# Gated linear attention into two mixture layers on one core: the transposed keys share pY's bank, POOL's selection comes after the state's scaling, the words of w_in are fetched later, and y has three buffers

## The chip, the cores and the metric

The kernel runs on one core of a Trainium2 chip. The metric is the device time of one execution in microseconds (us), and lower is better. The engines are named as in the profile: PE (TensorE, with PEld for its weight loads), DVE (VectorE), ACT (ScalarE), POOL (GpSimd) and SP (the queue that issues the DMAs). Each engine works through its own instructions in program order and waits on semaphores for the others.

## What is computed

The reference has three parts. The change lies in the first one and in the preparation of one weight of the third.

```python
# attention: B=4, H=8, S=768, D=48, a state of 48x48 per head
f = 1/(1+exp(-f_logit))
for t in range(S):
    state = f[t][:,None]*state + outer(k[t], v[t])
    y[t]  = q[t] @ state
x = y.transpose(0,2,1,3).reshape(3072, 384)
# first mixture layer: 8 experts, each takes its 384 best tokens
logits = x @ w_gate ; greedy assignment by logit ; out = relu(x@w1[e]) @ w2[e]
# second layer: one dense pair of weights
h = x @ w_in ; out = (h*clip(h+3,0,6)/6) @ w_out
```

## The kernel before

`gla_moe_ffn` first runs `attention` (until about 190 us of the span), then routes the tokens and runs eight experts, whose matmuls fill PE until the end.

**Units and chunks.** Attention cuts each batch's 768 steps into units of 384 and chunks of 128. There are 8 units and 24 chunks. A unit has three chunks, and one round of the main loop (lines 232 to 262) handles chunk j while it prepares a third of the next unit's data. A round with `ti==2` is the last of its unit: there POOL also rearranges the next unit's q and k (`reorder`, line 66), some 2.5 us each, and ACT its f (line 65).

**What a round does.** Four groups `tg(0)` to `tg(3)` each transpose one head pair of f, q or k into a bank pT (PE, line 81). ACT turns f into `ff` (line 85), and DVE makes running products `P` (93) and `S` (91) and scales q and k by them into `qt` (105) and `kh` (98). Between these groups stand the matmuls of the chunks:

- `l_mm(j-1)`, line 195: the finished y of the chunk before is transposed to rows and multiplied with w_gate, into bank pM. ACT copies `y` out (line 200), DVE reduces the logits `lg` (197), and SP stores y to x_dram (201). `y` has two buffers.
- `y_mm(j,0)`, line 163: the state `St` times q, into bank pY. The first chunk of a sequence has none.
- `a_mm(j+1)`, line 135: the next chunk's scores, into banks pA0 and pA1. ACT copies them to `am` (line 140), and POOL zeroes what lies after the step, with an affine select in place (line 141, `a_ev`).
- `y_mm(j,1)`, line 169: the scores times v, added in pY. ACT copies the result to `yt` (171).
- `kv_mm(j)`, line 181: the transposed keys `kt` times v, into pK. DVE adds that to the state (188, or 186 in the first chunk), POOL scales the state (189). This pair is the closure `update`, appended to the list `late`.
- `kt_mm(j+1)`, line 148: the keys of the next chunk are transposed into bank pM, and ACT copies them to `kt` (149). The last chunk of a sequence has none, so 20 of 24 rounds have one.

The function `group` runs what was left over from the group before, calls one step of `prep` as a filler, and at its end everything in `late`, in order. Eight banks of PSUM are in use: three pT, pA0, pA1, pM, pY and pK, one buffer each.

```python
            tg(0)
            if 0<=j-1<NCH: l_mm(j-1)
            tg(1)
            if 0<=j<NCH: y_mm(j,0)
            a_mm(j+1); a_ev(j+1,0); a_ev(j+1,1)
            if 0<=j<NCH: y_mm(j,1)
            if j>=0: kv_mm(j)
            tg(2)
            if j+1<NCH: kt_mm(j+1)
            tg(3)
```

**The preparation of w_in.** `narrowed` (from line 858) is a generator that is stepped by the groups. The weight arrives as 64-bit words, twelve blocks of 512 KB. For each block, ACT takes an absolute value into `pm` (line 872), DVE does four integer steps (882, 884, 886, 889), of which the last writes `pw`, ACT rounds to `wih` (line 669), and POOL subtracts for `wil` (line 670). `pw` has two buffers, and the block after next is fetched (line 867) at once behind that subtraction, whose end SP then awaits.

Of the kernel before, what the change touches and what calls it, by code (L numbers as in the profile page):

```python
# [10 lines left out]
F32=mybir.dt.float32; F32R=mybir.dt.float32r; BF=mybir.dt.bfloat16; I32=mybir.dt.int32; U32=mybir.dt.uint32  # L11
AF=mybir.ActivationFunctionType; OP=mybir.AluOpType; AX=mybir.AxisListType
PS=bass.MemoryType.PSUM
B,H,S,D=4,8,768,48
C=128; U=384; NP=4; NU=B*S//U; NCH=B*S//C
PMIN=2.0**-60; PB=3; MB=1

def attention(tc, q,k,v,f,wg, x_dram, lg, ident, pmin, ranges, prep, setup, spin):
    nc=tc.nc
    ctx=ExitStack()  # L20
    with ctx:
        ld=ctx.enter_context(tc.tile_pool(name="ald",bufs=2))
        cs=ctx.enter_context(tc.tile_pool(name="acs",bufs=1))
        wk=ctx.enter_context(tc.tile_pool(name="awk",bufs=2))
        ps=ctx.enter_context(tc.tile_pool(name="aps",bufs=1,space=PS))
# [42 lines left out]
        def tgroup(u,p,nm):  # L68
# [14 lines left out]
            if nm=='f':  # L83
# [3 lines left out]
                P2=PP[u,p//2]; P=P2[:,p%2]; pp=slice(p-1,p+1)  # L87
                V=nc.vector; ends=lambda t: t.rearrange("p a (c t) -> p a c t",t=C)[:,:,:,C-1]
                def suffix():
                    SS[u,p]=wk.tile([128,U],F32,name="S",bufs=3)  # L90
                    V.tensor_tensor_scan(SS[u,p][:,::-1],ff[:,1:U+1][:,::-1],m1[:,p%2,::-1],1.0,op0=OP.mult,op1=OP.max)
                SF[u,p]=suffix
                ops=[lambda: V.tensor_tensor_scan(P,m0,ff[:,:U],1.0,op0=OP.max,op1=OP.mult)]
                if p%2==0: return ops,[]
                return (ops+[lambda: V.tensor_scalar(PC[u][:,pp],ends(P2),PMIN,None,op0=OP.max)],
                        [lambda: V.reciprocal(ends(m1),PC[u][:,pp]),SF[u,p-1]])
            elif nm=='k':
# [38 lines left out]
        def a_ev(j,s):  # L136
            if s==0:
                AM[j]=wk.tile([128,2,NP,C],F32,name="am")
            am=AM[j][:,s]
            nc.scalar.copy(am,pA[j][s])  # L140
            nc.gpsimd.affine_select(out=am,in_=am,pattern=[[0,NP],[1,C]],compare_op=OP.is_ge,fill=0.0,base=0,channel_multiplier=-1)
        def kt_mm(j):
            u,c=divmod(j,3)
            if j%6==5: return
            kt=wk.tile([128,4,2,64],F32,name="kt")
            pk=ps.tile([128,NP,128],F32,name="pM",bufs=MB)
            for p in range(NP):
                nc.tensor.transpose(pk[:,p],KH[u][:,p,c*C:(c+1)*C],ident)
            nc.scalar.copy(kt.rearrange("p a s d -> p a (s d)"),pk)
            KT[j]=kt  # L150
# [22 lines left out]
        def kv_mm(j):  # L173
            u,c=divmod(j,3); first=j%6==0
            if j%6==5 or j>=NCH: return
            vr=raw['v',u]
            bank=ps.tile([128,512],F32,name="pK")
            pk=bank[:,:NP*D].rearrange("p (a d) -> p a d",a=NP)
            for p in range(NP):
                for s in range(2):  # L180
                    nc.tensor.matmul(pk[64*s:64*s+64,p],KT[j][:,p,s],vr[:,c,2*p+s,:D],start=True,stop=True)
            sn=St[(j+1)%2][:,:,:D]; so=St[j%2][:,:,:D]
            def update():
                pcb=PC[u][:,:,c][:,:,None].to_broadcast([128,NP,D])
                if first:
                    nc.vector.tensor_tensor(out=sn,in0=pk,in1=pcb,op=OP.mult)
                else:
                    nc.vector.tensor_add(so,so,pk)
                    nc.gpsimd.tensor_tensor(out=sn,in0=so,in1=pcb,op=OP.mult)
            late.append(update)  # L190
        def l_mm(j):
            W=2*D+8
            px=ps.tile([128,512],F32,name="pM" if j<NCH-1 else "pK",bufs=MB)[:,:NP*W].rearrange("p (a e) -> p a e",a=NP)
            for p in range(NP):
                nc.tensor.matmul(px[:,p],YT[j][:,p],SW[:,p],start=True,stop=True)  # L195
            y=wk.tile([128,NP,2*D],F32,name="y")
            def logits(): nc.vector.tensor_reduce(lg[:,j],px[:,:,2*D:].rearrange("p a e -> p e a"),axis=AX.X,op=OP.add)
            if j==NCH-1: logits()
            else: late.append(logits)
            nc.scalar.copy(y,px[:,:,:2*D])  # L200
            later.append(lambda: nc.sync.dma_start(x_dram[j*C:(j+1)*C,:],y.rearrange("p a d -> p (a d)")))
# [32 lines left out]
        for j in range(-1,NCH+1):  # L234
            tu,ti=divmod(j+1,3)
            tu+=1
            g=[(tu,)+x for x in ORD[4*ti:4*ti+4]] if tu<NU else [None]*4
            if j>=0 and j%3==0 and j//3+1<NU: load(j//3+1,'v')
            def tg(i):
                group(tgroup(*g[i]) if g[i] is not None else ([],[]),(lambda: next(prep,None)) if j>=0 and i in PREP[ti] else None,(ti,i)==(2,3))  # L240
            if j==NCH: spin(lambda: ps.tile([128,384],F32,name="pT",bufs=PB),TAIL[0])
            tg(0)
            if 0<=j-1<NCH: l_mm(j-1)
            if j==NCH: spin(lambda: ps.tile([128,384],F32,name="pT",bufs=PB),TAIL[1])
            tg(1)
            while later: later.pop(0)()
            if ti==2: refill(tu+1,'f')
            if 0<=j<NCH: y_mm(j,0)
            if j+1<NCH:
                a_mm(j+1)  # L250
                a_ev(j+1,0)
                a_ev(j+1,1)
            if 0<=j<NCH: y_mm(j,1)
            if j>=0: kv_mm(j)
            tg(2)
            if j+1<NCH: kt_mm(j+1)
            if ti==2: refill(tu+1,'q')
            tg(3)
            if ti==2: refill(tu+1,'k')
            if j>=0: next(constants,None)  # L260
            if j>=NCH-4: next(ranges,None)
            if j in (17,22,24): next(early)
            if 0<=j<10: next(prep,None)
# [54 lines left out]
class Routing:  # L318
# [60 lines left out]
    def spin(s,tile,n):  # L379

        if not n: return
        t=tile()
        for _ in range(n): s.tc.nc.tensor.matmul(t[:,:128],s.ones,s.before,start=True,stop=True)  # L383
# [23 lines left out]
    def phase(s,k):  # L407
        nc=s.tc.nc; V=nc.vector
        b24=lambda x: x[:,:,None].to_broadcast([128,NT,E])
# [258 lines left out]
def split_raw(nc, raw, hi, lo, eng_lo):  # L668
    nc.scalar.copy(hi, raw)  # L669
    eng_lo.tensor_tensor(out=lo, in0=raw, in1=hi.bitcast(F32), op=OP.subtract)  # L670
# [175 lines left out]
def gla_moe_ffn(tc,q,k,v,f_logit,moe_w_gate,moe_w1,moe_w2,moe2_w_in,moe2_w_out,out):  # L846
    nc=tc.nc
    with ExitStack() as ctx:
# [6 lines left out]
        nc.vector.memset(pmin,1.0)  # L855
        rwk=ctx.enter_context(tc.tile_pool(name="rwk",bufs=1))
        wih=cs.tile([128,3,F2],F32R,name="wih"); wil=cs.tile([128,3,F2],F32R,name="wil")
        def narrowed(pool,jobs,W,work,places):

            words=jobs[0].dtype!=F32  # L860
            got={}; mag={}
            def fetch(i):
                if i>=len(jobs): return
                n=jobs[i].shape[-1]
                w=pool.tile([128,W,2],U32,name="pw",bufs=2)
                if not words: w=w.rearrange("p c t -> p (c t)")[:,:n].bitcast(F32)
                nc.sync.dma_start(w.rearrange("p c t -> p (c t)") if words else w,jobs[i].bitcast(U32) if words else jobs[i])
                got[i]=w
            def absolute(i):
                if not words or i>=len(jobs): return  # L870
                mag[i]=work(i)
                nc.scalar.activation(mag[i],got[i][:,:,1].bitcast(F32),AF.Abs)
            fetch(0); fetch(1)
            yield
            absolute(0)
            for i in range(len(jobs)):
                yield
                r=got[i]
                if words:
                    V=nc.vector  # L880
                    lw,hw=got[i][:,:,0],got[i][:,:,1]; m=mag[i]; t=m.bitcast(U32)
                    V.tensor_scalar(m,m,2.0**-15,None,op0=OP.max)
                    yield
                    V.tensor_scalar(t,t,3,0x3ffffff8,op0=OP.logical_shift_left,op1=OP.bitwise_and)
                    yield
                    V.scalar_tensor_tensor(t,hw,0xC0000000,t,op0=OP.bitwise_and,op1=OP.bitwise_or)
                    yield
                    absolute(i+1)
                    V.scalar_tensor_tensor(lw,lw,29,t,op0=OP.logical_shift_right,op1=OP.bitwise_or)
                    r=lw.bitcast(F32)  # L890
                hi,lo=places(i)
                split_raw(nc,r,hi,lo,nc.gpsimd)
                fetch(i+2)
        def prep_in(pool):
            cc=lambda i: slice(i%4*512,i%4*512+512)
            return narrowed(pool,[moe2_w_in[i//4*128:i//4*128+128,cc(i)] for i in range(12)],512,
                            lambda i: pool.tile([128,512],F32,name="pm",bufs=2),
                            lambda i: (wih[:,i//4,cc(i)],wil[:,i//4,cc(i)]))
        wol={}
        def prep_out(pool):  # L900
            def places(g):
# [134 lines left out]
```

## Time and profile before

| | us |
|---|---|
| median of 3 runs | 896.9 (895.48 to 900.68) |
| the profiled execution | 900.39 |
| its span in the trace | 898.7 |
| PE busy over the span | 837.9 (93%) |
| DVE busy | 534.9 (60%) |
| ACT busy | 371.1 (41%) |
| POOL busy | 307.8 (34%) |
| granted clock of PE, mean | 0.968 |

The profile is of one execution. Busy shares are averages over attention, routing and experts, which have different limits, so what a change in attention is worth is read from the stretch of attention alone. The granted clock is given as a share: 1.00 is 2.4 GHz and 0.50 is 1.2 GHz. A row of the timeline gives the start in us from the span's start, the duration, the engine, the line, the operation and its tiles; in brackets stands the idle time of that engine just before the row, and what ended it.

### The profile page before, as it was taken

What the parts mean: (1) busy time and instruction counts of PE and PEld (TensorE: products, weight loads), DVE (VectorE), ACT (ScalarE), POOL (GpSimd) and SP (SyncE); (2) the same over time, 40 slices, a digit from 0 to 9 for tenths busy, and PEclk for the clock granted to TensorE, in tenths of its full rate; (3) what the DMA queues carried; (4) which work ended last, traced back from release to release, by engine and by line L of the source; (5) the groups of instructions that cost most, each with busy time, mean ns of one, the idle gap of its engine ahead of it and who ended that gap; (6) DMA issues with size and microseconds to landing.
All of it is one profiled execution on the core that took longest, in us unless ns stands there. A gap on an engine that the chain in (4) does not pass through costs nothing.

```text
span 898.7 us, 16095 instructions
## 1 busy us (share of the span) xinstructions
PE 837.9 (93%) x6086; PEld 788.9 (88%) x6086; DVE 534.9 (60%) x1369; ACT 371.1 (41%) x741; POOL 307.8 (34%) x378
## 2 busy tenths in 40 slices
PE   7998889896987699999999999999999999999995
PEld 5887778786877699989999999999999999999995
DVE  7989799567768844674574565555674422431331
ACT  4655556424234441542354144316423541642331
POOL 7677566316213540432133133313330440331001
PEclk9999899977999899999999999999999999999998
DMA  8775686026123411120221112201220220110000
GB/s 257 189 167 125 172 237 144 29 78 187 53 71 101 119 62 37 63 71 27 74 62 33 63 62 63 71 27 58 61 77 12 75 91 18 60 47 27 1 1 31
DMA packets 77158, 71.91 MB, mean 80 GB/s; under 512 B 29200, under 2 KB 65040, under 8 KB 77072
## 3 DMA queue, kind: packets, MB, share of 16 engines
q1 hardware_dynamic: 74000, 61.37, 24.0%
q0 software_dynamic: 3072, 9.44, 3.3%
q8 instruction: 49, 0.80, 0.4%
q14 instruction: 37, 0.30, 0.1%
HBM read 61.35 MB, written 9.44 MB: 79 GB/s over the span
## 4 chain that ended last, share of the span: by engine, by line
PE 57%; issue 14%; DVE 7%; ACT 2%; POOL 2%; DMA 2%; SPq 0%; POOLq 0%; ACTq 0%; DVEq 0%
PE pF L673 9%; PE acc L673 9%; PE pF L675 8%; PE pF L674 8%; PE acc L675 8%; PE acc L674 8%; POOL wol L670 1%; DVE ga L806 1%; PE pM L195 1%; PE pA L135 1%; DMA pw<-in_moe_w_out_dram 1%; PE pY L169 1%; PE pY L163 1%; PE acc L383 1%; POOL out_dram L838 1%
## 5 line engine op out<-in xcount | busy, mean ns | idle before, releaser
L806 DVE SCALAR_TENSOR_TENSOR ga<-ga,pF 128x384 f32<-128x384 f32 x128 | 70.7, 552 | 109.5 <-ACT ga L805 109.3
L673 PE MATMUL pF<-xh,wih 128*128 128x384 f32 x384 | 133.3, 347 | 1.9 <-ACT xh L790 1.9
L673 PE MATMUL acc<-woh,hh 128*128 128x384 f32 x384 | 134.2, 349 | 0.0
L675 PE MATMUL pF<-xl,wih 128*128 128x384 f32 x384 | 131.3, 342 | 0.0
L674 PE MATMUL pF<-xh,wil 128*128 128x384 f32 x384 | 130.9, 341 | 0.0
L674 PE MATMUL acc<-woh,hl 128*128 128x384 f32 x384 | 130.0, 339 | 0.9 <-DVE hl L809 0.9
L675 PE MATMUL acc<-wol,hh 128*128 128x384 f32 x384 | 130.0, 338 | 0.0
L670 POOL TENSOR_TENSOR w1l<-wst,w1h 128x512 fp32r<-128x512 f32 x42 | 55.6, 1323 | 173.9 <-ACT w1h L669 173.9
L805 ACT ACTIVATE ga<-pF,three 128x384 f32<-128x384 f32 x128 | 74.1, 579 | 99.2 <-PE pF L675 99.1
L809 DVE TENSOR_TENSOR hl<-ga,hh 128x384 fp32r<-128x384 f32 x128 | 72.8, 569 | 60.2 <-ACT hh L808 59.9
L808 ACT CAST hh<-ga 128x384 fp32r<-128x384 f32 x128 | 65.7, 513 | 104.0 <-DVE ga L806 104.0
L670 POOL TENSOR_TENSOR w2l<-wst,w2h 128x384 fp32r<-128x384 f32 x58 | 59.9, 1035 | 111.5 <-ACT w2h L669 111.5
L771 ACT ACTIVATE hh<-pF 128x384 fp32r<-128x384 f32 x64 | 31.4, 492 | 123.1 <-PE pF L675 111.9
L772 DVE SCALAR_TENSOR_TENSOR hl<-pF,hh 128x384 fp32r<-128x384 f32 x64 | 35.5, 555 | 75.1 <-ACT hh L771 74.8
L673 PEld LDWEIGHTS pF<-xh,wih 128*128 128x128 f32 x384 | 73.0, 190 | 2.3 <-ACT xh L790 2.2
L674 PEld LDWEIGHTS acc<-woh,hl 128*128 128x128 f32 x384 | 72.7, 189 | 1.3 <-DVE hl L809 1.3
L675 PEld LDWEIGHTS pF<-xl,wih 128*128 128x128 f32 x384 | 73.3, 191 | 0.4 <-DVE xl L791 0.3
L674 PEld LDWEIGHTS pF<-xh,wil 128*128 128x128 f32 x384 | 73.2, 191 | 0.0
L673 PEld LDWEIGHTS acc<-woh,hh 128*128 128x128 f32 x384 | 72.7, 189 | 0.1
L675 PEld LDWEIGHTS acc<-wol,hh 128*128 128x128 f32 x384 | 72.6, 189 | 0.0
L673 PE MATMUL pF<-xh,w1h 128*128 128x384 f32 x192 | 67.8, 353 | 0.6 <-ACT xh L741 0.6
L675 PE MATMUL acc<-hl,w2h 128*128 128x384 f32 x192 | 64.5, 336 | 3.0 <-DVE hl L772 3.0
(286 smaller groups left out, 1766.8 us busy)
## 6 DMA issues: line engine op xcount, KB each, us to landing
wst<-in_moe_w_dram SPq DMA_DIRECT2D x58, 192.0 KB, 2.4
wst<-in_moe_w_dram SPq DMA_DIRECT2D x42, 256.0 KB, 2.7
pw<-in_moe_w_in_dram SPq DMA_DIRECT2D x12, 512.0 KB, 4.0
pw<-in_moe_w_out_dram SPq DMA_DIRECT2D x16, 384.0 KB, 3.1
v<-in_v_dram SPq DMA_DIRECT2D x24, 192.0 KB, 5.2
x_dram<-y SPq DMA_DIRECT2D x24, 192.0 KB, 3.6
fr<-in_f_logit_dram SPq DMA_DIRECT2D x7, 576.0 KB, 5.4
kr<-in_k_dram SPq DMA_DIRECT2D x7, 576.0 KB, 5.6
```

The source lines that it names most:

```text
L135: nc.tensor.matmul(pA[j][s][:,p],KH[u][r,p,c*C:(c+1)*C],QT[u][r,p,c*C:(c+1)*C],start=True,stop=True)
L163: for r in rows: nc.tensor.matmul(PY[j][p//2][r,p],St[j%2][r,p],QT[u][r,p,cc],start=p==0 or last and p==2,stop=False)
L670: eng_lo.tensor_tensor(out=lo, in0=raw, in1=hi.bitcast(F32), op=OP.subtract)
L673: nc.tensor.matmul(out, ahi, bhi, start=start, stop=False)
L674: nc.tensor.matmul(out, alo, bhi, start=False, stop=False)
L675: nc.tensor.matmul(out, ahi, blo, start=False, stop=stop)
L771: nc.scalar.activation(hh,p,AF.Relu)
L772: s.defer(2,lambda: nc.vector.scalar_tensor_tensor(hl,p,0.0,hh.bitcast(F32),op0=OP.max,op1=OP.subtract))
L805: nc.scalar.activation(a,p,AF.Relu,bias=s.three[:,0:1])
L806: late(f,1,lambda: nc.vector.scalar_tensor_tensor(g,a,6.0,p,op0=OP.min,op1=OP.mult))
L808: late(f,1,lambda: nc.scalar.copy(gh,g))
L809: late(f,3,lambda: nc.vector.tensor_tensor(out=gl,in0=g,in1=gh.bitcast(F32),op=OP.subtract))
```

## The change

There are four edits. `kt_mm` moves from the end of a round (for the next chunk) to the next round, behind `tg(0)` and ahead of `l_mm`, and its transposes go into bank pY and not into pM. The affine select is no longer issued in `a_ev` but put into `late`, and `update` goes to the front of `late`, so that POOL scales the state first. The words of w_in's block i+1 are fetched when the work on block i begins, which is one step of the generator later than before. `y` gets a third buffer.

```diff
@@ a_ev
             nc.scalar.copy(am,pA[j][s])
-            nc.gpsimd.affine_select(out=am,in_=am,pattern=[[0,NP],[1,C]],compare_op=OP.is_ge,fill=0.0,base=0,channel_multiplier=-1)
+            late.append(lambda: nc.gpsimd.affine_select(out=am,in_=am,pattern=[[0,NP],[1,C]],compare_op=OP.is_ge,fill=0.0,base=0,channel_multiplier=-1))
@@ kt_mm
-            pk=ps.tile([128,NP,128],F32,name="pM",bufs=MB)
+            pk=ps.tile([128,NP,128],F32,name="pY")
@@ kv_mm
-            late.append(update)
+            late.insert(0,update)
@@ l_mm
-            y=wk.tile([128,NP,2*D],F32,name="y")
+            y=wk.tile([128,NP,2*D],F32,name="y",bufs=3)
@@ the loop over the rounds
             tg(0)
+            if 0<=j<NCH: kt_mm(j)
             if 0<=j-1<NCH: l_mm(j-1)
...
             tg(2)
-            if j+1<NCH: kt_mm(j+1)
             if ti==2: refill(tu+1,'q')
@@ narrowed, which prep_in now calls with after=True
                 if words:
                     V=nc.vector
+                    if after and i>0: fetch(i+1)
...
                 split_raw(nc,r,hi,lo,nc.gpsimd)
-                fetch(i+2)
+                if not (words and after): fetch(i+2)
```

POOL, from the last round of one unit into the first round of the next (76 to 91 us in the trace), before (St is the state, am the scores, pmq and pmk the rearranged q and k, r_before a constant and wil the block of w_in):

```order
L670 TENSOR_TENSOR wil<-pw,wih 128x512
L141 AFFINE_SELECT am<-am 128x512 x2
L189 TENSOR_TENSOR St_114<-St_116,pc 128x4x48
L66 TENSOR_SCALAR pmq<-qr 128x8x48 x3
L66 TENSOR_SCALAR pmk<-kr 128x8x48 x3
L346 MEMSET r_before 128x128
L347 AFFINE_SELECT r_before<-r_before 128x128
L670 TENSOR_TENSOR wil<-pw,wih 128x512
L141 AFFINE_SELECT am<-am 128x512 x2
L189 TENSOR_TENSOR St_116<-St_114,pc 128x4x48
```

and now:

```order
L670 TENSOR_TENSOR wil<-pw,wih 128x512
L189 TENSOR_TENSOR St_114<-St_116,pc 128x4x48
L141 AFFINE_SELECT am<-am 128x512 x2
L66 TENSOR_SCALAR pmq<-qr 128x8x48 x3
L66 TENSOR_SCALAR pmk<-kr 128x8x48 x3
L346 MEMSET r_before 128x128
L347 AFFINE_SELECT r_before<-r_before 128x128
L670 TENSOR_TENSOR wil<-pw,wih 128x512
L189 TENSOR_TENSOR St_116<-St_114,pc 128x4x48
L141 AFFINE_SELECT am<-am 128x512 x2
```

In each round the two selects changed places with the scaling; the rearranging of q and k stands behind both, as before.

ACT, from one `yt` copy to the next round's scores (pA), in a round with groups of f and a block of w_in, before:

```order
L171 COPY yt<-pY 128x512
L149 COPY kt<-pM 128x512
L85 ACTIVATE ff_118<-pT,half 128x384
L872 ACTIVATE pm<-pw 128x512
L669 CAST wih<-pw 128x512
L200 COPY y<-pM 128x384
L85 ACTIVATE ff_120<-pT,half 128x384
```

and now:

```order
L171 COPY yt<-pY 128x512
L85 ACTIVATE ff_118<-pT,half 128x384
L872 ACTIVATE pm<-pw 128x512
L669 CAST wih<-pw 128x512
L149 COPY kt<-pY 128x512
L200 COPY y<-pM 128x384
L85 ACTIVATE ff_120<-pT,half 128x384
```

The copy of the keys moved behind what the groups issue in between, here `ff`, `pm` and `wih`.

PE, one of the last rounds, which have no groups any more, before:

```order
L169 MATMUL pY<-am,v_108 64x128 x8
L181 MATMUL pK<-v_108,kt 64x48 x8
L148 MATMUL pM<-ident,kh_113 128x128 x4
L195 MATMUL pM<-sw,yt 128x104 x4
L163 MATMUL pY<-qt,St_116 64x128 x8
```

and now:

```order
L169 MATMUL pY<-am,v_108 64x128 x8
L181 MATMUL pK<-v_108,kt 64x48 x8
L148 MATMUL pY<-ident,kh_113 128x128 x4
L195 MATMUL pM<-sw,yt 128x104 x4
L163 MATMUL pY<-qt,St_116 64x128 x8
```

The order here is the same; only the bank changed, so that the transposes follow the reading of pY by `yt`, and line 163 follows the reading of pY by `kt`.

## Rows read from the trace of the kernel before

**Rows 1.** Windows, attention's main part: busy us of each engine, clock, DMA.

```profile
core 0: us, PE busy (x) PEld busy (x) DVE busy (x) ACT busy (x) POOL busy (x), PEclk, DMA share, GB/s
22.00:164.00 142.00, 129.37 (x1600) 112.59 (x1602) 128.94 (x233) 82.17 (x160) 92.40 (x138) 0.96 0.65 166
```

**Rows 2.** Waits of DVE, 22 to 165 us: total, times, longest.

```profile
DVE St L188 <- PE pK L181: 6.4, 3, 3.5
```

**Rows 3.** Timeline, POOL, PE and DVE around the first late scaling.

```profile
42.63 2.34 POOL L141 TENSOR_SCALAR_AFFINE_SELECT am<-am 128x512 f32<-128x512 f32 x2
...
45.68 1.97 PE L163 MATMUL pY<-qt,St 64*64 64x128 f32 x16 [1.54 <-POOL St L189]
...
51.04 0.35 DVE L188 TENSOR_TENSOR St<-St,pK 128x192 f32<-128x192 f32 x1 [2.29 <-PE pK L181]
```

**Rows 4.** Timeline, the same engines around the second late scaling.

```profile
78.91 1.43 POOL L141 TENSOR_SCALAR_AFFINE_SELECT am<-am 128x512 f32<-128x512 f32 x2 [0.78 <-ACT am L140]
...
79.66 0.34 DVE L188 TENSOR_TENSOR St<-St,pK 128x192 f32<-128x192 f32 x1
...
81.75 1.09 PE L163 MATMUL pY<-qt,St 64*64 64x128 f32 x16
...
87.90 2.06 POOL L141 TENSOR_SCALAR_AFFINE_SELECT am<-am 128x512 f32<-128x512 f32 x2
...
89.93 1.14 POOL L189 TENSOR_TENSOR St<-St,pc 128x192 f32<-128x192 f32 x1
...
91.13 1.97 PE L163 MATMUL pY<-qt,St 64*64 64x128 f32 x16 [2.61 <-POOL St L189]
...
97.58 0.35 DVE L188 TENSOR_TENSOR St<-St,pK 128x192 f32<-128x192 f32 x1 [3.47 <-PE pK L181]
```

**Rows 5.** Windows, two us behind the second late scaling (columns as in rows 1).

```profile
92.00:94.00 2.00, 2.00 (x20) 1.67 (x18) 1.97 (x5) 0.00 (x0) 0.00 (x0) 0.50 1.05 308
```

**Rows 6.** Timeline, ACT and PE in the round from 72 us.

```profile
72.42 0.67 ACT L872 ACTIVATE pm<-pw 128x512 f32<-128x512 f32 x1
...
74.04 1.09 PE L163 MATMUL pY<-qt,St 64*64 64x128 f32 x16
...
76.06 0.68 ACT L669 CAST wih<-pw 128x512 fp32r<-128x512 f32 x1 [2.98 <-DVE pw L889]
...
77.08 0.62 PE L181 MATMUL pK<-v,kt 128*64 128x48 f32 x16
```

**Rows 7.** Timeline, ACT and DVE in the round from 80 us.

```profile
82.86 0.67 ACT L669 CAST wih<-pw 128x512 fp32r<-128x512 f32 x1
...
86.16 0.34 DVE L188 TENSOR_TENSOR St<-St,pK 128x192 f32<-128x192 f32 x1
```

**Rows 8.** Timeline, ACT, PE and DVE in the round from 133 us.

```profile
135.75 1.09 PE L163 MATMUL pY<-qt,St 64*64 64x128 f32 x16
135.78 0.58 ACT L85 ACTIVATE ff<-pT,half 128x384 f32<-128x384 f32 x1 [1.48 <-DVE S L91]
...
137.13 0.69 ACT L669 CAST wih<-pw 128x512 fp32r<-128x512 f32 x1 [0.19 <-DVE pw L889]
...
140.70 0.34 DVE L188 TENSOR_TENSOR St<-St,pK 128x192 f32<-128x192 f32 x1
```

**Rows 9.** Timeline, POOL and DVE at the fourth unit's rearranging.

```profile
103.37 1.66 POOL L141 TENSOR_SCALAR_AFFINE_SELECT am<-am 128x512 f32<-128x512 f32 x2 [1.25 <-ACT am L140]
...
108.51 0.17 DVE L360 TENSOR_SCALAR q_mi<-q_mi 128x4 int32<-128x4 int32 x1 [2.48 <-POOL q_mi L359]
```

**Rows 10.** Timeline, ACT and PE, the last round that transposes keys.

```profile
177.32 0.58 ACT L171 COPY yt<-pY 128x512 f32<-128x512 f32 x1
...
177.60 0.66 PE L148 MATMUL pM<-ident,kh 128*128 128x128 f32 x4
...
178.99 1.14 PE L195 MATMUL pM<-sw,yt 128*128 128x104 f32 x8 [0.62 <-ACT kt L149]
```

**Rows 11.** Waits of SP in attention, then one load and its reader.

```profile
SPq L867 <- POOL wil L670: 42.5, 9, 8.5
...
78.16 0.34 SPq L867 DMA_DIRECT2D pw<-in_moe_w_in_dram  x1
...
82.25 0.69 ACT L872 ACTIVATE pm<-pw 128x512 f32<-128x512 f32 x1 [1.23 <-DMA pw<-in_moe_w_in_dram]
```

More of the change, by code (lines that the diff above doesn't have):

```diff
@@ L857, in gla_moe_ffn, with narrowed @@
         wih=cs.tile([128,3,F2],F32R,name="wih"); wil=cs.tile([128,3,F2],F32R,name="wil")
-        def narrowed(pool,jobs,W,work,places):
+        def narrowed(pool,jobs,W,work,places,after=False):
             words=jobs[0].dtype!=F32
@@ L897, in prep_in @@
                             lambda i: pool.tile([128,512],F32,name="pm",bufs=2),
-                            lambda i: (wih[:,i//4,cc(i)],wil[:,i//4,cc(i)]))
+                            lambda i: (wih[:,i//4,cc(i)],wil[:,i//4,cc(i)]),True)
         wol={}
```

## The prediction

> **What bounds the kernel now.** I read the windows by stage first. In attention's main part, 22 to 164 us, DVE is busy 128.9 of 142 us and PE 129.4 [rows 1], so both are close to full, and neither can gain much without the other. All four edits lie in attention; what follows it runs the same instructions in the same order, so I take its length as fixed and ask only by how much attention ends earlier or later. Because DVE is nearly full and its list of work does not change, the test for a step is whether DVE's idle time grows or shrinks. PE's own waits count only where they reach DVE.
>
> The waits of DVE come next. The largest is the addition to the state (line 188) waiting for the product of keys and values: 6.4 us in 3 places, the longest 3.5 [rows 2]. The timeline shows where two of them come from. POOL runs in order, and at the change of a unit it has the rearranging of q and k, a block of w_in and the two selects ahead of the state's scaling. `y_mm(j,0)` then waits: 1.54 us at 45.68 [rows 3] and 2.61 us at 91.13 [rows 4]. After each pause those 16 matmuls take 1.97 us instead of 1.09 [rows 3, 4], since the granted clock is at 0.50, the 1.2 GHz level [rows 5]. So the state's next addition comes late, and DVE idles 2.29 us [rows 3] and 3.47 us [rows 4].
>
> **The change, part by part.**
>
> *Scaling ahead of the selects.* At the second place two selects (2.06 us) leave the chain ahead of the scaling, but those of the round before (1.43 us) now stand behind their own scaling and so enter it [rows 4]: the scaling comes 0.6 us earlier, not 2. With POOL's other rows unchanged `y_mm(j,0)` starts near 90.5, and PE's wait is split, as the rearranged k is late too and PE waits for that first. I take the clock to stay high then. A full-clock round goes from `y_mm(j,0)` to the end of `kv_mm` in 3.66 us (74.04 to 77.70 [rows 6]), so the product is there at 94.2. DVE came to its wait at 97.58-3.47=94.11 [rows 4]. **Gain 3.4 us.** At the first place the same sum gives 2.34-1.43=0.9 us earlier [rows 3, 4], 44.8, and the product at 48.4, before DVE asks for it at 48.75: **gain 2.3 us**. If the clock fell there all the same, only the 0.6 and 0.9 us would be left; these are the lower ends.
>
> The other side of it: a select can no longer run while DVE still works on the state's addition. Where a unit changes, the rearranging begins later by up to one pair of selects. In most rounds that has slack. At 108.51 it has none: DVE waits 2.48 us for a constant that POOL issues behind the rearranging, and the selects that now stand between took 1.66 us [rows 9]. They can't start before the scaling has ended. **Loss 1.5 us**, between 1.2 (two selects at their fastest, half the 2.34 of [rows 3]) and 1.7.
>
> *Keys transposed later, into pY's bank.* The wait of `l_mm` for the copy `kt` goes. Of its sum, the last rounds get something back, since there DVE is idle and PE's chain sets the end. Here the transposes must wait for `yt`, until 177.90, and `l_mm` can follow at about 178.5 instead of 178.99 [rows 10]: 0.5 us in each of two rounds. **Gain 1.0 us.** In the main part the wait that goes was PE's alone.
>
> In its place comes a new wait. pY is needed again by `y_mm(j,0)`, and that must wait until ACT has copied `kt` out. ACT is in order, and the copy now stands behind the `ff`, `pm` and `wih` that the groups issued, of which `ff` waits for a DVE scan and `wih` for DVE's last step on the words. Of the 20 rounds with keys, most have these early enough. Three have not:
>
> - From 72 us: `wih` waits 2.98 us for DVE and ends at 76.74 [rows 6]. A copy of this size takes 0.58 us [rows 10], so `y_mm(j,0)` starts at 77.4 and not at 74.04. The product is there at 77.4+3.66=81.1, and DVE, which asks at 79.66 [rows 4], idles **1.4 us**.
> - From 80 us: `wih` ends at 83.53 [rows 7], the copy at 84.15, and `y_mm(j,0)` starts 2.4 us later than 81.75 [rows 4]. The product comes at 87.8 against 86.16 [rows 7]. **Loss 1.65 us.**
> - From 133 us: `ff` waits for DVE until 135.78 and `wih` ends at 137.82, so `y_mm(j,0)` starts at 138.45 instead of 135.75, and the product comes at 142.1 against 140.70 [rows 8]. **Loss 1.4 us.**
>
> These are pauses of PE of 3.4, 2.4 and 2.7 us, as long as those behind which the clock fell [rows 3, 4, 5]. A fall costs what the second late scaling shows: 6.45 us from `y_mm(j,0)` to the state's addition (91.13 to 97.58 [rows 4]) instead of 3.66 and a little, so 2.7 us. I count one fall, at the longest pause: **loss 2.7 us**. The ends are none and three.
>
> *Words later, third buffer.* I cost both at nothing. SP already waits 42.5 us over 9 loads until POOL has let the buffer go [rows 11]; a load issued one step later mostly waits for the same subtraction. The cover is the time until ACT reads: one load was issued at 78.16 and its reader stood at 82.25, having waited 1.23 us [rows 11]. A load that slips by more than such slack stalls ACT, and with it `kt`. The Trainium skill, "DMA: Bandwidth & Descriptors", Rules for kernel authors, says to issue a DMA early and wait on it late, which speaks against this edit. By it, each of ten loads would pay such a wait; the trace shows that wait once at this size, and the sum by the rule is the last rival. The third buffer frees `y` from waiting for a store; `y` is read by nothing but the store, so the wait that goes has nothing behind it but ACT's slack (82.2 busy of 142 us [rows 1]).
>
> **The sum.** Gains 3.4+2.3+1.0=6.7. Losses 1.5+1.4+1.65+1.4+2.7=8.65. Net 2.0 us longer: the profiled execution, 900.39 us with a span of 898.7, would become 902.4, and on the scale of the runs, whose median of 896.9 lies 3.5 below it, **898.9 us**. A measurement of this kernel can tell about 0.5% from no change, 4.5 us, that is below 892.4 or above 901.4. So I forecast no difference that can be told.
>
> **The rivals.**
>
> *The new wait does not bite.* ACT's late rows are late because of DVE; with 5.7 us of DVE's idle time gone, its scans and word steps come earlier against PE, and `kt` is copied in time. Then only the gains and the rearranging count: 6.7-1.5=5.2 us shorter, **891.7 us**. For it: at 72 us PE itself runs late behind DVE. Against it: the waits of DVE [rows 2] leave DVE one further, small wait of this kind, so what sets when `wih` can start is hardly shortened ahead of the three rounds. Chance 0.31.
>
> *The new wait halves the clock each time (the slower side).* PE's pauses before `y_mm(j,0)` take the place of those for the scaling: three in place of two. It decides from pauses of some 2.4 us on; one of 1.54 us was already followed by slow matmuls [rows 3]. Then 8.65+2x2.7=14.05 against 6.7: 7.3 us longer, **904.2 us**. For it: the lengths. Against it: each of these pauses comes straight behind transposes and `l_mm`. Chance 0.24.
>
> *The words come late.* Ten loads with 1.23 us each on ACT ahead of `kt` and `am` would be 12 us, on top of the forecast **911 us**. Against it: after the first 22 us the windows show DMA busy 0.65 [rows 1], and SP's waits say that the buffer decides, not the place in the program. Chance 0.03.
>
> *The change does not do what it says*, as the wait for `kt` only turns into one for `yt`, and the scaling only moves by 0.6 and 0.9 us: gains 2.5, with the 1.5 lost, **895.9 us**. This lies in the forecast's own range, 893 to 901.4, and I give the two together 0.42.
>
> **How the numbers follow.** Forecast 0.42, copies in time 0.31, three falls of the clock 0.24, late words 0.03. So faster by over 0.5% 0.31, within 0.5% 0.42, slower 0.27. The bounds reach from 6.7-1.2=5.5 us shorter (891.4, with small waits of DVE down to 889) to 1.7+4.45+8.1 less the lower gains of 2.5, 11.8 us longer. The range for 8 in 10 is 889 to 906: it leaves out the late words, the worst sum, and a gain above what DVE's two idle places hold.
>
> **What would show it.** Right: DVE's waits for the product at 51 and 97 us gone or under 1 us; new waits of PE at line 163 for ACT's `kt` (line 149), 2 to 3.5 us each in three rounds, and a granted clock of about 0.5 behind at least one; DVE's wait for the constant near 4 us; `l_mm` without waits for `kt`. Wrong: no such waits at line 163 (then the first rival), ACT waiting for w_in's blocks at line 872 over 1.5 us in many rounds (the last but one), or attention's end moved by more than 6 us either way, or a change of the time with attention's end where it was, which would mean that routing or the experts moved.

## The result, and the profile after

| | before | after |
|---|---|---|
| median of the runs, us | 896.52 (895.48 to 900.68) | 910.46 (908.49 to 911.07) |
| the profiled execution, us | 900.39 | 908.49 |
| its span, us | 898.7 | 906.7 |
| busy in the span, us: PE, DVE, ACT, POOL | 837.9, 534.9, 371.1, 307.8 | 838.6, 538.2, 371.1, 307.9 |
| granted clock, mean | 0.968 | 0.964 |

The ratio is 1.0147 (95% interval 1.0115 to 1.018): slower, by 13.9 us between the medians, outside the range of 889 to 906 and on the other side of the bound of 0.5%. The two profiled executions differ by only 8.1 us, since the one of before lies near the longest of its runs and the one of after is the shortest. The traces account for the 8.1; the other 5.8 us are seen only in medians, those of the experiments included.

Busy time is the same on PE, ACT and POOL, within 0.7 us, and 3.3 us longer on DVE, whose instructions are the same 1369; the rest is waiting. The windows of attention's main part, in the columns of [rows 1], and four of its stretches, after:

```profile
22.00:164.00 142.00, 122.36 (x1476) 107.98 (x1477) 120.52 (x212) 77.67 (x151) 86.50 (x134) 0.93 0.62 161
77.00:83.00 6.00, 5.71 (x50) 5.16 (x52) 2.08 (x4) 2.94 (x7) 1.13 (x1) 0.50 0.61 175
89.00:93.00 4.00, 4.00 (x47) 3.60 (x45) 2.08 (x4) 1.49 (x3) 3.90 (x6) 0.65 0.69 174
118.00:124.00 6.00, 5.65 (x35) 5.09 (x37) 5.93 (x14) 2.35 (x6) 1.49 (x3) 0.50 1.01 227
144.00:149.00 5.00, 4.25 (x42) 3.83 (x44) 2.30 (x4) 1.85 (x5) 1.65 (x1) 0.66 1.11 258
```

Against [rows 1], DVE did 8.4 us less work in the same 142 us, and PE 7.0 us less. The clock is at its lower level for all or most of four stretches; before, it was so behind the two late scalings.

**Where the time goes.** Line 188 adds the product of keys and values to the state (186 in the first chunk of a sequence), once in every round that has keys and in the same order in both kernels. So its rows are a clock of progress. In the timeline of DVE before (rows not among those above):

```profile
72.63 0.34 DVE L186 TENSOR_TENSOR St<-pK,pc 128x192 f32<-128x192 f32 x1
...
104.57 0.36 DVE L188 TENSOR_TENSOR St<-St,pK 128x192 f32<-128x192 f32 x1 [0.15 <-PE pT L81]
...
119.53 0.34 DVE L186 TENSOR_TENSOR St<-pK,pc 128x192 f32<-128x192 f32 x1
...
132.82 0.35 DVE L188 TENSOR_TENSOR St<-St,pK 128x192 f32<-128x192 f32 x1 [0.60 <-PE pK L181]
...
171.75 0.35 DVE L188 TENSOR_TENSOR St<-St,pK 128x192 f32<-128x192 f32 x1 [2.92 <-PE pK L181]
```

and after:

```profile
50.24 0.35 DVE L188 TENSOR_TENSOR St<-St,pK 128x192 f32<-128x192 f32 x1 [0.24 <-PE pK L181]
...
72.67 0.34 DVE L186 TENSOR_TENSOR St<-pK,pc 128x192 f32<-128x192 f32 x1
83.82 0.35 DVE L188 TENSOR_TENSOR St<-St,pK 128x192 f32<-128x192 f32 x1 [4.09 <-PE pK L181]
94.08 0.35 DVE L188 TENSOR_TENSOR St<-St,pK 128x192 f32<-128x192 f32 x1 [2.70 <-PE pK L181]
100.98 0.35 DVE L188 TENSOR_TENSOR St<-St,pK 128x192 f32<-128x192 f32 x1
109.22 0.36 DVE L188 TENSOR_TENSOR St<-St,pK 128x192 f32<-128x192 f32 x1 [0.64 <-PE pT L81]
125.58 0.36 DVE L186 TENSOR_TENSOR St<-pK,pc 128x192 f32<-128x192 f32 x1 [0.40 <-PE pK L181]
...
138.59 0.35 DVE L188 TENSOR_TENSOR St<-St,pK 128x192 f32<-128x192 f32 x1 [0.79 <-PE pK L181]
...
150.12 0.35 DVE L188 TENSOR_TENSOR St<-St,pK 128x192 f32<-128x192 f32 x1 [3.25 <-PE pK L181]
...
182.16 0.35 DVE L188 TENSOR_TENSOR St<-St,pK 128x192 f32<-128x192 f32 x1 [2.99 <-PE pK L181]
```

The lag of after behind before, in these rows: -0.8 us at the first late scaling [rows 3], 0.0 at 72, then +4.2 (83.82 against 79.66 [rows 4]), +7.9 (against 86.16 [rows 7]), +3.4 behind the second late scaling (100.98 against 97.58 [rows 4]), +4.65 (109.22), +6.05 (125.58), +5.8 (138.59 against 132.82), +9.4 (150.12 against 140.70 [rows 8]) and +10.4 (182.16). So it is lost in three jumps of 4.1, 3.8 and 3.65 us (the last between 139 and 150) and in smaller steps of 0.8 to 1.4; 4.5 us are won back once. At attention's end, the last `l_mm`, the lag is 9.2 us (196.46 against 187.28); what follows is 1.2 us shorter than before.

The three jumps stand where the prediction put the late key copies. PE's rows at line 163 with a wait for `kt`, in the timeline after:

```profile
77.29 1.97 PE L163 MATMUL pY<-qt,St 64*64 64x128 f32 x16 [3.14 <-ACT kt L149]
...
88.70 1.09 PE L163 MATMUL pY<-qt,St 64*64 64x128 f32 x16 [2.17 <-ACT kt L149]
89.73 1.69 PE L135 MATMUL pA<-qt,kh 64*128 64x128 f32 x16
91.35 1.97 PE L169 MATMUL pY<-am,v 128*64 128x128 f32 x16
...
105.10 1.09 PE L163 MATMUL pY<-qt,St 64*64 64x128 f32 x16 [1.46 <-ACT kt L149]
...
144.75 1.96 PE L163 MATMUL pY<-qt,St 64*64 64x128 f32 x16 [3.20 <-ACT kt L149]
```

and ACT ahead of the first and the last of them:

```profile
76.09 0.66 ACT L669 CAST wih<-pw 128x512 fp32r<-128x512 f32 x1 [2.89 <-DVE pw L890]
76.65 0.59 ACT L149 COPY kt<-pY 128x512 f32<-128x512 f32 x1
...
143.47 0.65 ACT L669 CAST wih<-pw 128x512 fp32r<-128x512 f32 x1 [1.78 <-DVE pw L890]
144.02 0.58 ACT L149 COPY kt<-pY 128x512 f32<-128x512 f32 x1
```

The chain reads from ACT to PE to DVE and back: `wih` waits for DVE's last step on the words, the copy stands behind `wih`, PE stops ahead of `y_mm(j,0)`, the 16 matmuls behind the stop take 1.97 us instead of 1.09 (and in the second place the next ones do), and DVE waits 4.09, 2.70 and 3.25 us for the product. A fourth stop, at 105.10, the prediction hadn't listed.

### The profile page after: what moved, and what is told of

It reads as the page before. It is cut to its first block, busy times and chain, and to the rows that moved or that the text cites. A ratio compares the mean times of both kernels' runs of the same rounds, so it can differ in the third digit from the quotient of the medians.

```text
span 906.7 us, 16127 instructions
## 1 busy us (share of the span) xinstructions
PE 838.6 (92%) x6086; PEld 791.1 (87%) x6086; DVE 538.2 (59%) x1369; ACT 371.1 (41%) x741; POOL 307.9 (34%) x378
## 4 chain that ended last, share of the span: by engine, by line
PE 60%; issue 16%; DVE 10%; POOL 6%; ACT 3%; DMA 3%; SPq 0%; POOLq 0%; ACTq 0%; DVEq 0%
PE pF L673 9%; PE acc L673 8%; PE pF L675 8%; PE pF L674 8%; PE acc L675 8%; PE acc L674 8%; PE pA L135 2%; PE pY L163 1%; PE pY L169 1%; PE pT L81 1%; PE pM L195 1%; POOL wol L670 1%; DMA pw<-in_moe_w_out_dram 1%; POOL pmq L66 1%; DVE P L93 1%
```

## The experiments

"Before" was measured anew beside each set: 898.19 us for the first four kernels, 897.17 for the next four, 897.14 for the last four. Ratios are to it, with 95% intervals; edits are against the changed kernel, except for those headed "before with", which are against before. Each kernel has one trace, of one execution.

**Which edit costs.** Four kernels: all but the keys, and each edit by itself.

```diff
 e1_keys_back: the change without
-            if 0<=j<NCH: kt_mm(j)
...
+            if j+1<NCH: kt_mm(j+1)
...
+            pk=ps.tile([128,NP,128],F32,name="pM",bufs=MB)
```

```diff
 e2_keys_alone: before with
-            pk=ps.tile([128,NP,128],F32,name="pM",bufs=MB)
+            pk=ps.tile([128,NP,128],F32,name="pY")
...
+            if 0<=j<NCH: kt_mm(j)
...
-            if j+1<NCH: kt_mm(j+1)
```

```diff
 e3_select_alone: before with
+            late.append(lambda: nc.gpsimd.affine_select(out=am,in_=am,pattern=[[0,NP],[1,C]],compare_op=OP.is_ge,fill=0.0,base=0,channel_multiplier=-1))
...
-            late.append(update)
+            late.insert(0,update)
```

```diff
 e4_fetch_buffer: before with
+                    if after and i>0: fetch(i+1)
...
+            y=wk.tile([128,NP,2*D],F32,name="y",bufs=3)
```

> The change without its first edit: the keys are again transposed at the end of the round before, into pM; selects behind the scaling, later words and third buffer stay. Theory K (the copy kt stands behind ff and wih on ACT, and y_mm(j,0) waits for it): all of the loss goes, and as the scaling comes earlier the kernel is 0 to 5 us faster than before (891 to 897). Theory S (the selects push the rearranging of q and k): most of the loss stays, 903 to 910. Theory W (late words): the loss stays, 905 to 910.

> The kernel before with the first edit alone (keys transposed in the next round, into pY). Theory K: about as slow as the whole change, 905 to 912, with waits of PE at line 163 for kt of 2 to 3.5 us in three or four rounds. Theory S: as before, 894 to 899. Theory W: as before.

> The kernel before with the second edit alone (selects in the late list, scaling first). Theory K: 891 to 897, the two long waits of y_mm(j,0) for the scaling at most 1 us each, DVE's wait for the constant near 4 us. Theory S: 903 to 910, with waits of PE for the rearranged k of 1 us and more.

> The kernel before with later words and the third buffer alone. Theories K and S: within 2 us of before (894.5 to 898.5). Theory W: 903 to 910, with waits of ACT at line 872 for the words of over 1 us in more than five blocks.

| kernel | us | ratio |
|---|---|---|
| e1_keys_back | 896.55 | 0.998 (0.9966 to 0.9994) |
| e2_keys_alone | 903.03 | 1.0053 (1.0034 to 1.0072) |
| e3_select_alone | 897.07 | 0.9995 (0.998 to 1.0011) |
| e4_fetch_buffer | 897.98 | 0.9993 (0.9978 to 1.0009) |

Without the keys edit everything comes back, so that edit is needed for the loss. But alone it costs 0.53%, some 5 us, and the others alone nothing that these runs can tell, which leaves about 9 of the 14 us to the keys in company with another edit.

**Which company.** The keys with one of the other two:

```diff
 e7_keys_select: the change without
-                    if after and i>0: fetch(i+1)
...
-            y=wk.tile([128,NP,2*D],F32,name="y",bufs=3)
+            y=wk.tile([128,NP,2*D],F32,name="y")
```

```diff
 e8_keys_fetch_buffer: the change without
-            late.append(lambda: nc.gpsimd.affine_select(out=am,in_=am,pattern=[[0,NP],[1,C]],compare_op=OP.is_ge,fill=0.0,base=0,channel_multiplier=-1))
+            nc.gpsimd.affine_select(out=am,in_=am,pattern=[[0,NP],[1,C]],compare_op=OP.is_ge,fill=0.0,base=0,channel_multiplier=-1)
...
-            late.insert(0,update)
+            late.append(update)
```

> The change without the later fetch and the third buffer: keys and selects. The keys alone cost some 5 us (903.0 against 898.2), selects, fetch and buffer alone nothing, all four 14. So about 9 us come from the keys together with another edit. Theory P (the selects join): with the keys late the state's addition is late, and the selects that now stand behind the scaling make the scores late as well, or push the rearranging once more: about 909 us here, more waits of DVE at line 188 than the 10.7 us of the keys alone, and PE waits at line 81 for the rearranged keys. Theory F (the fetch joins): w_in's words come later, so DVE's last step on them and ACT's rounding come later, with the key copy behind them: here only the 903 us of the keys alone.

> The change without the selects edit: keys, later fetch and third buffer. Theory F (the fetch joins): about 909 us, ACT waiting for words or for DVE's last step on them longer than the 12.3 us of the keys alone, and PE's waits at line 163 for the key copy over 10 us. Theory P (the selects join): 903 us, as the keys alone. If both this and the kernel of keys and selects lie between 905 and 908, each joins with a part.

With the selects 908.35 us, 1.0129 (1.0098 to 1.016); with fetch and buffer 904.39, 1.0083 (1.0057 to 1.0109). The first is theory P's. Its trace runs beside that of the whole change within 0.1 us in every round of attention (the last `yt` copy at 192.64 against 192.55), so beside the selects the later fetch and the third buffer move nothing in attention. The second lies between the two theories by its median, 0.3% above the keys alone, and the two intervals overlap. Its trace, in which attention ends 1.4 us sooner than with the keys alone (the last `yt` at 186.57 against 187.95), is of the shortest of its six runs, and so can't settle whether the fetch adds up to 0.3% to the keys.

**Why the copy is late.** Three ways to place the transposes, with all other edits kept:

```diff
 e15_keys_first
+            if 0<=j<NCH: kt_mm(j)
             tg(0)
-            if 0<=j<NCH: kt_mm(j)
```

```diff
 e5_old_place_pY
-            if 0<=j<NCH: kt_mm(j)
...
             tg(2)
+            if j+1<NCH: kt_mm(j+1)
```

```diff
 e9_keys_in_pK
-            pk=ps.tile([128,NP,128],F32,name="pY")
+            pk=ps.tile([128,512],F32,name="pK").rearrange("p (a d) -> p a d",a=NP)
```

> All edits, same bank pY, same round, but the key transposes stand ahead of the first group and not behind it, so that the copy stands directly behind yt on ACT, ahead of the group's ff, pm and wih. Theory K (the copy waits behind ff and wih): PE's waits at line 163 for line 149 fall from 10.0 us to under 2, and the time to 897 to 900. Rival B (sharing pY in the round itself): the waits stay over 5 us, 905 or more. A price that both expect: the transposes stand sooner behind yt and may wait for it at line 148 as they do at their old place (10.5 us in 11 places there, at no cost in time).

> All edits, but the key transposes stand at their old place behind the third group of the round before; only their bank is pY. Theory K (the copy's place in ACT's queue, behind ff and wih, ahead of the state product): the copy is out long before the state product needs the bank, no waits of PE at line 163 for line 149 over 0.7 us, within 1.5 us of the change without the keys edit, 896 to 898. Rival B (the bank itself: two users of pY in turn make the wait wherever the transposes stand): 903 us or more, with the waits at line 163 as in the change.

> All edits, the key transposes at their new place, but into bank pK and not pY: the state product no longer waits for the copy, only the product of keys and values does, some 2 to 3 us further down PE's order. Theory K (PE stops at the state product because the bank is shared): most of the 14 us come back, 897 to 901, and the granted clock stays at 1.00 in most windows. Rival L (the late copy is what costs, whichever instruction waits for it): 903 to 910, with PE waiting at line 181 for line 149 in place of line 163. A third way: the transposes now wait for DVE's addition to the state, which reads pK, ahead of everything else in PE's round: PE waits at line 148 for line 188, 1 to 2 us in many rounds, 905 or more.

| kernel | us | ratio |
|---|---|---|
| e15_keys_first | 898.52 | 1.0014 (0.9999 to 1.0029) |
| e5_old_place_pY | 897.03 | 0.9995 (0.9981 to 1.001) |
| e9_keys_in_pK | 900.67 | 1.0032 (1.0015 to 1.0049) |

PE's waits from 22 to 164 us (total, times, longest), with the transposes ahead of the first group:

```profile
PE pY L148 <- ACT yt L171: 7.3, 6, 3.3
PE pY L163 <- ACT kt L149: 1.6, 1, 1.6
```

in pK (from 22 to 175 us):

```profile
PE pK L148 <- DVE St L186: 5.4, 4, 1.9
PE pK L148 <- DVE St L188: 1.7, 3, 0.6
```

and in the change:

```profile
PE pY L163 <- ACT kt L149: 10.0, 4, 3.2
```

Same bank, same round; only the transposes moved ahead of the first group, and with them the copy to an earlier place in ACT's queue: 12 of the 14 us come back. PE still waits 8.9 us for ACT there, but 7.3 of them for `yt`, which stands early in ACT's order, and DVE waits for the product of keys and values 1.1 us at line 188 and 1.2 at line 186, against 12.3 and 0.4 in the change. So neither the bank by itself nor the round was the fault; it was that the copy stood behind `ff` and `wih` while PE's next instruction needed the bank. In pK that wait is gone as well, with the copy as late as ever (at 77.73, 4.0 us behind the addition at 73.74; in the change 76.65 and 72.67); the transposes now wait for DVE, as the third of the expectations had it, but at a price of 3 us and not of 8 or more. The Trainium skill, "Perfetto Trace Analysis", Optimizing Tensor Performance, says that independent groups of matmuls should rotate through different banks, so that the copying out of one overlaps the next; the 10.0 us agree with it, and the 0.9995 of the old place in the same bank shows that sharing cost nothing here where the reader is early.

**What the clock costs.** Extra matmuls on a constant fill PE's stops in the four rounds.

```diff
 e14_fill
+            if j in {7:14,8:10,10:8,15:14}: warm({7:14,8:10,10:8,15:14}[j])
             if 0<=j<NCH: y_mm(j,0)
```

> All edits, and in the four rounds in which the state product waits for the key copy, PE gets 14, 10, 8 and 14 extra transposes of a constant block into pK (0.15 us each, 2.1, 1.5, 1.2 and 2.1 us) ahead of that product, fewer than its wait holds. Their results are not used. Theory C (each pause costs twice: by itself, and by the slow clock behind it): the product's matmuls stay at 1.09 us in these rounds and not 1.97, 4 to 6 us are given back, about 905. Rival (only the pause itself costs, PE has slack behind it): the clock stays high and the time stays within 1.5 us of 910. If the clock falls all the same, the extra work was too short, and the time stays too.

903.43 us, 1.0067 (1.0047 to 1.0087): 0.8% of the 1.47% given back, 7 us, for *more* work on PE. One block took 0.24 us and not 0.15 (28 instructions for 14 blocks, where a key transpose takes one), so the stops were filled to the end. The timeline, PE and DVE:

```profile
73.82 3.29 PE L217 MATMUL pK<-ident 128*128 128x128 f32 x28
77.15 1.09 PE L163 MATMUL pY<-qt,St 64*64 64x128 f32 x16
...
80.86 0.35 DVE L188 TENSOR_TENSOR St<-St,pK 128x192 f32<-128x192 f32 x1 [1.26 <-PE pK L181]
...
89.54 0.35 DVE L188 TENSOR_TENSOR St<-St,pK 128x192 f32<-128x192 f32 x1 [1.13 <-PE pK L181]
...
144.47 0.35 DVE L188 TENSOR_TENSOR St<-St,pK 128x192 f32<-128x192 f32 x1 [1.67 <-PE pK L181]
```

and the windows that answer to the four of after:

```profile
77.00:83.00 6.00, 5.96 (x87) 5.50 (x86) 4.12 (x9) 3.96 (x10) 2.71 (x5) 1.00 0.56 167
85.00:89.00 4.00, 4.00 (x64) 3.59 (x64) 2.69 (x5) 2.45 (x6) 3.92 (x7) 1.00 0.47 132
114.00:120.00 6.00, 5.93 (x37) 5.38 (x39) 5.93 (x13) 2.35 (x6) 1.21 (x3) 0.50 0.96 221
140.00:145.00 5.00, 4.91 (x77) 4.41 (x76) 2.73 (x7) 2.99 (x7) 1.72 (x2) 1.00 1.04 252
```

`y_mm(j,0)` starts no sooner: at 77.15 against 77.29, and in the other two rounds 4.91 and 6.18 us behind the state's addition before it (85.77 and 140.70), against 4.88 and 6.16 in the change. Yet DVE's three waits shrink from 4.09+2.70+3.25=10.04 us to 1.26+1.13+1.67=4.06, and the three jumps of the lag from 11.5 us to 5.6. So by these traces 6.0 us of the loss are the clock behind the stops, and 4.1 of the waits are the stops themselves. Three of the four slow stretches are gone; the one at 114 us, which has another cause, shown next, stays.

**What the selects add.** In the change, POOL, DVE, ACT and PE at the constant `q_mi`:

```profile
110.12 1.22 POOL L141 TENSOR_SCALAR_AFFINE_SELECT am<-am 128x512 f32<-128x512 f32 x2
...
114.33 0.17 DVE L360 TENSOR_SCALAR q_mi<-q_mi 128x4 int32<-128x4 int32 x1 [3.67 <-POOL q_mi L359]
...
115.34 0.65 ACT L669 CAST wih<-pw 128x512 fp32r<-128x512 f32 x1 [2.88 <-DVE pw L890]
...
116.91 0.55 PE L81 MATMUL pT<-ident,pmf 128*128 128x128 f32 x3 [1.87 <-ACT ff L85]
...
121.70 2.08 PE L135 MATMUL pA<-qt,kh 64*128 64x128 f32 x16
```

The selects stand ahead of the rearranging and so of the constant; DVE's wait for it is 3.67 us against 2.48 [rows 9], `wih`, `y` and `ff` follow late, PE stops 1.87 us for `ff`, and the clock falls. Two kernels issue that constant one step sooner, one from the change, one from the change without its keys edit:

```diff
 e12_const_early, and e13_keys_back_const on e1_keys_back
         G.tensor_scalar(s.sel,t,1.0,0.0,op0=OP.mult,op1=OP.add)
-        yield
         s.mask=c("mask",[128,4],F32); w=s.t("mi",[128,4],I32)
         G.iota(w,pattern=[[-1,4]],base=4,channel_multiplier=1)
+        yield
```

> All edits, and the constant q_mi is issued on POOL one round earlier, ahead of the selects and the rearranging. Theory P2 (what the selects add to the keys comes in part over that constant: DVE waits 3.67 us for it, so the last step on the words, wih, y and ff come late one after the other, PE stops 1.87 us and its clock falls): DVE's wait is gone, the slow matmuls from 118 to 124 us too, 3 to 5 us given back, about 906. Rival: the wait only moves to another row of DVE, since the rounds there wait for the keys, 909 to 911.

> The change without its keys edit, with the constant q_mi issued one round earlier. Theory P2: DVE's wait of 3.67 us is gone, 1.5 to 3 us less than the 896.6 of the change without the keys edit: 893.5 to 895, a ratio of about 0.996 to the kernel before. Rival: that wait is hidden behind others there and the time stays within 0.5 us of 896.6.

906.37 us, 1.0096 (1.0078 to 1.0115), and 895.29 us, 0.9975 (0.9958 to 0.9993). In the first, DVE's wait for the constant is gone and so is the fall of the clock behind it; the place now reads:

```profile
116.96 0.49 PE L81 MATMUL pT<-ident,pmf 128*128 128x128 f32 x3
117.38 1.16 PE L135 MATMUL pA<-qt,kh 64*128 64x128 f32 x16
```

By the ratios that is 0.5% of the 1.47%, some 4.5 us, and was expected at 3 to 5. The traces put less of it at the constant. In the change the lag grows by 1.4 us from 109.22 to 125.58; here it shrinks by 0.2 in the same stretch (108.12 and 122.86), so the constant is worth 1.6 us. The slow clock behind it cost little, since DVE was busy for 5.93 of the 6 us from 118. Another 1.1 us of the difference stood there already in the round from 72 us, ahead of the constant, where the clock was low for a shorter time and DVE waited 2.82 us instead of 4.09. The fill and this edit were not run together. The second kernel has the lowest median of all, 0.25% below before, but only 1.3 us below the change without its keys edit, where 1.5 to 3 were expected, and their intervals overlap: that the constant is worth something there is not shown.

By the traces the keys alone end attention 4.6 us sooner than the change (the last `l_mm` at 191.86 against 196.46): 1.4 us at the constant, 1.2 up to 72 us and 1.7 in the round of the second jump. The last part was not the selects'. In that round `y_mm(j,0)` waits 2.17 us in the change and the matmuls behind it slow down (88.70 above), while with the keys alone, after 2.02 us, they stay fast:

```profile
87.50 1.09 PE L163 MATMUL pY<-qt,St 64*64 64x128 f32 x16 [2.02 <-ACT kt L149]
88.52 1.16 PE L135 MATMUL pA<-qt,kh 64*128 64x128 f32 x16
```

But with the keys, fetch and buffer, again without the selects edit, the same stop is followed by slow matmuls:

```profile
86.22 1.09 PE L163 MATMUL pY<-qt,St 64*64 64x128 f32 x16 [2.02 <-ACT kt L149]
87.23 2.02 PE L135 MATMUL pA<-qt,kh 64*128 64x128 f32 x16
```

Of the 1.2 us up to 72 us, 0.8 go with a cost that no wait shows. DVE's busy time over the span is 534.4 to 535.6 us in the four traces without the selects edit and 537.6 to 540.1 in the ten with it, always for 1369 instructions; its four integer steps on the words take 37.0 us in the change against 34.6 before. Between the additions at 50 and 72 us DVE waits for nothing, before or in the change, and still the lag grows by 0.8 us; with the keys alone it doesn't grow. Why the same instructions take longer when the selects stand behind the scaling is not shown.

## Why the prediction was wrong

**The step that failed** is the size of one term: "I count one fall, at the longest pause: loss 2.7 us". In the profiled execution all three pauses brought a fall, and together the falls cost 6.0 us by the filled kernel; in the four other traces with the late copy and unfilled stops, two or three of the pauses brought one. So the three jumps of the lag came to 11.5 us, where 4.45+2.7=7.15 were forecast. The argument that kept it at one, that each pause comes straight behind transposes and `l_mm`, had no row behind it, and [rows 3] spoke the other way: a stop of 1.54 us followed by matmuls of 1.97.

**The pauses themselves were right.** 1.4+1.65+1.4=4.45 us were forecast, in those three rounds; with the clock kept up DVE waited 4.06. The rule used, when does ACT end `wih` and when does DVE ask, held; PE's own stops, forecast at 3.4, 2.4 and 2.7 us, were 3.14, 2.17 and 3.20. It missed the round at 105 us (1.46 us of PE, a step of 1.25 us in the lag), which I had not gone through.

**The constant was right in size.** DVE's wait was forecast near 4 us and was 3.67; the loss was forecast at 1.5 us, and the lag grew by 1.4 in the change and by 1.6 against the kernel with the early constant. What the prediction left out about the selects is the longer work of DVE: it took DVE's list of work as unchanged, and the list is, but its time grew by 3.3 us.

**The gains were added up, and don't add.** The second scaling's 3.4 us did come (4.5 us of lag won back). But with the keys alone, selects as before, the lag shrinks by 4.4 us at the same place: `y_mm(j,0)` stops 0.59 us there, for `kt` (94.52), and DVE waits 0.84 us at 98.29, against 3.47 before. Both edits remove the same wait, so in company the selects bring little but their cost. The first scaling's 2.3 us were 0.8 and had run out by 72 us; with only fetch and buffer, without the selects edit, 1.6 us came at that place too, as the clock did not fall there. The tail's 1.0 was about 1.2 (the lag goes from 10.4 to 9.2 between 182 us and the last `l_mm`).

**Words and buffer at nothing** held: 0.9993. The Trainium skill's advice to issue a DMA early ("DMA: Bandwidth & Descriptors", Rules for kernel authors) came to no price that these runs can tell: the last rival's 12 us did not come, and ACT's waits for the words from 22 to 164 us were 3.0 us in the change, 2.3 in the kernel with keys and selects, which fetches as before, and 1.5 before.

**The rivals.** The second, three falls and 904.2, was the one that happened, at 0.24. Its 7.3 us, against the 9.2 us of attention, lacked the fourth pause and counted the first scaling's gain, which did not last; three falls at 2.7 us each were more than the 6.0 measured. On the scale of the medians it still falls 6 us short; the medians of before and after differ by about that much more than the two profiled executions do, and that part stays open. The first rival, copies in time, is refuted by the 10.0 us at line 163.

## What to carry to other kernels

When an edit moves a copy that frees a PSUM bank, write down what stands ahead of it in its engine's queue, round by round, and where PE first needs the bank; the same bank was free with the copy first in the queue and cost 12 us with it behind work that waits for DVE. Price each stop of PE twice, for its length and for the slow clock that may follow, and let the range hold all the falls that are possible: here like stops went either way. Before adding up gains, ask of each wait whether another part of the change removes it too, and follow each delay until an engine with idle time takes it up.

## What was not expected of the hardware

The length of a stop alone didn't say whether the clock falls; the same round went either way in different executions. In the round from 42 us a stop of 1.54 us was followed by matmuls of 1.97 us before [rows 3], and with only fetch and buffer a stop of 1.53 us was not:

```profile
45.37 1.09 PE L163 MATMUL pY<-qt,St 64*64 64x128 f32 x16 [1.53 <-POOL St L189]
46.39 1.16 PE L135 MATMUL pA<-qt,kh 64*128 64x128 f32 x16
```

In the round of the second jump 2.02 us went both ways (87.50 and 86.22 above). In the round of the third, 3.20 us in the change slowed the matmuls, and 3.07 us with keys, fetch and buffer didn't:

```profile
140.08 1.09 PE L163 MATMUL pY<-qt,St 64*64 64x128 f32 x16 [3.07 <-ACT kt L149]
141.10 1.16 PE L135 MATMUL pA<-qt,kh 64*128 64x128 f32 x16
```

There DVE waited 1.66 us for the product, as in the filled kernel (1.67), against 3.25 in the change. The runs of before fit this: of the 76 beside the three sets, those with a mean granted clock under 0.970 have medians of 898.1 to 898.7 us, set by set, the others 895.8 to 896.6. What decides whether the clock falls is left open. That idle PE is better given useless matmuls was the surprise in size: 7 us of 14.
